# A chunked delta-rule attention with a top-1 expert layer behind it: the chunk loop as one written list, all triangular inverses in halves, routing for four chunks at a time

## The chip, the cores and the metric

One core of one Trainium2 chip. The metric is the time on the device in microseconds, from the first to the last instruction of one launch, as the median of several executions.

## What is computed

Inputs r, k, v, w, a, b have the shape 4 x 8 x 768 x 40 (batch, head, step, width). For each of the 32 (batch, head) pairs a 40 x 40 state runs over the 768 steps; the output of a step is read before its update:

```python
y[:, :, t] = np.einsum('bhd,bhde->bhe', rt, state)
Sa = np.einsum('bhde,bhe->bhd', state, at)
state = state * wt[:, :, None, :] - np.einsum('bhd,bhe->bhde', Sa, bt) + np.einsum('bhd,bhe->bhde', vt, kt)
```

The 3072 rows y (320 wide, all heads of a step side by side) go through a mixture of experts: `logits = x @ w_gate`, the largest of 8 logits picks one expert, and the output row is its softmax weight times `relu(x @ w1[e]) @ w2[e]`, with hidden width 1024.

## The kernel before

**Attention.** The 768 steps are cut into 24 chunks of 32. Two batches share the partitions (rows 0 to 39 and 64 to 103), and 16 pairs lie side by side in the free dimension. One chunk needs these stages; the letters are those of the orders in the code.

- Preparation `p` (`prep`): `scan` (L224, VectorE) makes running products of the decays, `inv` (L229, L230, ScalarE) their reciprocals by Ln and Exp, `gmul` (L241, L242, VectorE) refines these into G, `kbmul` (L235) scales k and b, and `qmul` (L246) makes Q from a and G; these last two run on GpSimd. It also issues the loads of the next chunk's W, k/b and a on SyncE's queue.
- Gram blocks `E` (`estage`, L255, TensorE): products of the scaled k, b with Q; ScalarE copies them out (`m2` L263, `m1` L275, L276), GpSimd masks half of them (L281).
- Inversion `tops`: for four chunks together, 32 x 32 unit triangular matrices, one for each pair and chunk, are inverted on VectorE. For the first four chunks only the two 16 x 16 diagonal halves are inverted so, in 14 steps of two operations (L309, L311), and TensorE joins them (`tbd`, L337, L347). For the other five groups all 32 rows are done in 30 steps of two operations (L301, L303). A copy puts each chunk's inverses into a block-diagonal tile TBD (L331, ScalarE).
- The recurrence, chunk after chunk: `R` (`rhs`, L375) multiplies the state with Q, ScalarE copies (L378), `U` (`ustage`, L385) applies the inverses, ScalarE copies (L390), `S` (`sstage`, L402) makes the next state, VectorE scales it out of PSUM into SVR (L408), and `R` of the next chunk reads that.
- Output: transposes `K` (L360), `T` (L415) and `u` (L425), products `A` (L441, masked by VectorE in L444) and `y` (L463, scaled into xT in L469).
- Routing, for two chunks at a time: `r` (`route_a`) makes the logits and the token rows, `b` (`route_b`) the ranks within each expert; two indirect DMAs on GpSimd (L538) scatter the rows, each behind the one before it, to a table Xs in DRAM that is laid out by expert.

Chunks 0 to 3 are issued by the list `START`, in which `wn` stands for n products on the constant `scn` whose result nobody reads. From chunk 4 on each chunk is issued by the one-line `ORDER`, with shares of the inversion steps between its stages; there the framework's scheduler may still move instructions within its own model of time. `YW` and `AW` put more products on `scn` before `y` and `A` (L448). All engines work off their queues in order.

**Experts.** For each of 8 experts, 448 rows are read from Xs and transposed, weights and rows are split into a high and a low part, and TensorE does the two layers (`l1` L877 to L882, `l2` L897 to L905). In `l1`, the last third of the contraction is 64 rows deep: L880 covers high weight times high and low row (stacked in x2), and L882 adds low weight times high row, two column blocks side by side on the upper and the lower 64 rows of the array. Results are scaled (L910, or L907 and L908 for the last 64 rows) and scattered to the output by an indirect DMA (L911). At the end a check of the decays and the expert counts decides whether a slow general path is needed, which is not the case here.

Of the kernel before, what the change touches and what calls it, by code (L numbers as in the profile page):

```python
# [42 lines left out]
START = ("W0 s0 l0 j0 W1 s1 a1 a0 w22 c0 k1 w12 l1 g0 Q0 g1 W2 s2 l2 q1 W3 s3 w9 c5 g2 a2 q2 l3 e0 w3 n0 e1 k2 w1 W4 "  # L43
# [9 lines left out]
ENGS = {mybir.EngineType.PE, mybir.EngineType.Activation, mybir.EngineType.DVE, mybir.EngineType.Pool,  # L53
        mybir.EngineType.SP}
INIT = {0: (0, 1), 1: (2, 3, 4), 2: (5, 6)}
AALT = 4
I0 = 4
# [4 lines left out]
NKB, NG = 9, 10  # L62


def prepare(inputs):
# [7 lines left out]
    W = np.zeros((NC, 80, 16, C + 1), f32)  # L73
    W[..., 1:] = em(w)
# [4 lines left out]
    VR[..., 0:40], VR[..., 64:104] = V[..., 0::2, :], V[..., 1::2, :]  # L79
# [36 lines left out]
    d["cq"] = np.broadcast_to((ii[None] == (jj % C)[:, None])[:, None, 0:16], (128, 8, 16)).astype(f32)  # L116
# [7 lines left out]
def attention(tc, nc, d, ctx, Xs, okt, sent):  # L124
# [325 lines left out]
    def ystage(c):  # L450
# [7 lines left out]
        for js in ((0, 1),) if c < NC - 1 else ((0,), (1,)):  # L458
# [6 lines left out]
            if js[0] == 0:  # L465
                yield
# [621 lines left out]
```

## Time and profile before

| what | value |
|---|---|
| median of 3 runs | 705.46 us (701.49 to 706.08) |
| profiled execution | 701.49 us, its span 701.5 us |
| busy share of the span | TensorE 86%, VectorE 76%, ScalarE 60%, GpSimd 33% |
| first product of stage U of chunk 0 / of chunk 23 | 65.1 us / 438.1 us |
| first product of the experts | 464.85 us |
| granted TensorE clock, mean | 0.879 |

The profile gives for each engine the busy time, and for groups of instructions the mean duration and what ended the idle time before them. Times in the views by stage are microseconds from the start of the span. TensorE's records are pipelined and overlap, so that its busy time is not the same as work at full rate.

### The profile page before, as it was taken

The numbers are of one execution on the slowest core, as the hardware profiler recorded it, in microseconds if no ns is written. First come the engines' busy times: TensorE is split into PE (matmuls) and PEld (weight loads), VectorE is DVE, ScalarE is ACT, GpSimd is POOL, SyncE is SP. The second block draws the span as 40 slices with busy tenths as digits, with TensorE's granted clock in tenths as the row PEclk, the third lists the DMA queues.
The fourth block names the chain that finished last, engine by engine and source line by source line (L and its number), as shares of the span: only waits on it lengthen the run. The fifth ranks groups of instructions, "written<-read, shape, count | busy, mean of one in ns | idle before, by whom it ended". The sixth has DMA issues, their size and how long they took to land. (4 is left out here: it accounts for less than half of the span.)

```text
span 701.5 us, 25718 instructions
## 1 busy us (share of the span) xinstructions
PE 601.3 (86%) x10942; PEld 510.3 (73%) x10942; DVE 535.8 (76%) x1074; ACT 422.9 (60%) x962; POOL 228.7 (33%) x239
## 2 busy tenths in 40 slices
PE   7477786877978877868889899889999999999994
PEld 3345565766867676757778788758898898988984
DVE  7999699998999999999789634558657576485531
ACT  2565755678759867978786887445535445355320
POOL 5860534546545544457312101200111101201101
PEclk9788767897877788888889989869999999999998
DMA  6484457253434343424224332886454464552100
GB/s 200 119 210 121 141 180 254 75 161 111 123 103 121 103 122 103 133 90 129 78 82 128 111 93 82 243 245 212 134 174 127 145 220 129 168 189 74 56 1 31
DMA packets 48207, 93.26 MB, mean 133 GB/s; under 512 B 11577, under 2 KB 28090, under 8 KB 48024
## 3 DMA queue, kind: packets, MB, share of 16 engines
q1 hardware_dynamic: 45528, 83.65, 39.9%
q0 software_dynamic: 2560, 7.92, 3.2%
q8 instruction: 88, 1.44, 0.9%
q14 instruction: 31, 0.25, 0.1%
HBM read 78.98 MB, written 13.21 MB: 131 GB/s over the span
## 5 line engine op out<-in xcount | busy, mean ns | idle before, releaser
L911 POOL DMA_INDIRECT out<-yo,tok x32 | 30.8, 964 | 207.6 <-DVE yo L910 149.8
L301 DVE TENSOR_TENSOR tmp<-Mt,Tt 128x30 f32<-128x30 f32 (+9 forms) x150 | 79.7, 532 | 2.8
L303 DVE TENSOR_TENSOR Tt<-Tt,tmp 128x30 f32<-128x30 f32 (+9 forms) x150 | 77.1, 514 | 3.2
L886 DVE SCALAR_TENSOR_TENSOR hx<-m_hp,hx 128x384 fp32r<-128x384 f32 (+1 forms) x128 | 41.0, 383 | 34.9 <-ACT hx L884 34.9
L246 POOL TENSOR_TENSOR Q<-AT,G 128x1024 f32<-128x1024 f32 x18 | 50.3, 2796 | 40.9 <-DVE G L242 14.0
L884 ACT ACTIVATE hx<-m_hp 128x448 fp32r<-128x448 f32 x64 | 31.4, 543 | 49.0 <-PE m_hp L882 44.8
L897 PE MATMUL m_yp<-w2h,hx 128*128 128x320 f32 x192 | 61.0, 317 | 0.0
L899 PE MATMUL m_yp<-w2h,hx 128*128 128x320 f32 x192 | 59.1, 308 | 0.0
L898 PE MATMUL m_yp<-w2l,hx 128*128 128x320 f32 x192 | 59.1, 308 | 0.0
L402 PE MATMUL ps_r<-SVS,KS 128*40 128x40 f32 x1472 | 49.8, 228 | 9.3 <-ACT SVS L390 6.2
L364 ACT COPY KS<-ps_g 64x416 f32<-64x416 f32 x96 | 48.1, 501 | 14.8 <-PE ps_g L360 10.0
L281 POOL TENSOR_SCALAR_AFFINE_SELECT Q<-Q 32x512 f32<-32x512 f32 x44 | 38.1, 865 | 57.4 <-ACT Q L275 50.1
L255 PE MATMUL ps_g<-Q,KB 128*64 128x64 f32 x768 | 38.4, 273 | 20.9 <-POOL Q L246 10.5
L463 PE MATMUL psY<-Y,KS 128*40 128x32 f32 x1504 | 50.4, 221 | 5.2 <-DVE Y L444 4.3
L402 PEld LDWEIGHTS ps_r<-SVS,KS 128*40 128x40 f32 x1472 | 44.1, 141 | 12.3 <-ACT SVS L390 8.6
L255 PEld LDWEIGHTS ps_g<-Q,KB 128*64 128x64 f32 x768 | 34.4, 183 | 25.5 <-POOL Q L246 11.9
L331 ACT COPY TBD<-Tc 32x256 f32<-32x256 f32 x80 | 50.8, 635 | 3.2 <-DVE Tc L314 1.3
L463 PEld LDWEIGHTS psY<-Y,KS 128*40 128x40 f32 x1504 | 44.9, 142 | 10.0 <-DVE Y L444 6.7
L408 DVE TENSOR_TENSOR SVR<-ps_r,F 40x320 f32<-40x320 f32 x92 | 44.9, 488 | 8.8 <-PE ps_r L402 6.2
L877 PE MATMUL m_hp<-x,w1h 128*128 128x448 f32 x128 | 50.1, 391 | 0.4 <-ACT x L860 0.4
L538 POOL DMA_INDIRECT Xs<-xr,si x24 | 27.9, 1164 | 61.5 <-ACT TBD L331 15.9
L878 PE MATMUL m_hp<-x,w1h 128*128 128x448 f32 x128 | 47.7, 373 | 0.0
(187 smaller groups left out, 1555.2 us busy)
## 6 DMA issues: line engine op xcount, KB each, us to landing
w2r<-in_w SPq DMA_DIRECT2D x8, 1280.0 KB
w1r<-in_w SPq DMA_DIRECT2D x8, 1024.0 KB
VU<-in_VT SPq DMA_DIRECT2D x48, 160.0 KB
SVR<-in_VR SPq DMA_DIRECT2D x48, 104.0 KB
SVS<-in_VS SPq DMA_DIRECT2D x24, 208.0 KB
KB<-in_KB SPq DMA_DIRECT2D x30, 160.0 KB
KB<-in_KBP SPq DMA_DIRECT2D x9, 512.0 KB
Xs<-xr SPq DMA_DIRECT2D x7, 648.0 KB
```

Of the source, the lines that this page charges most:

```text
L246: eng.tensor_tensor(at(Q, s), buf(s)[3], g, ALU.mult)
L255: TE.matmul(e[j][:, x], kb[:, p, :], q[:, :, p, :], start=True, stop=True, tile_position=(0, 64 * j))
L301: V.tensor_tensor(t, Mt[:, 0:j, j:j + 1].broadcast_to([128, j, n]), Tt[:, j:j + 1, j + 1:32].broadcast_to([128, j, n]), ALU.mult)
L303: V.tensor_tensor(Tt[:, 0:j, j + 1:32], Tt[:, 0:j, j + 1:32], t, ALU.subtract)
L331: A.copy(o[bb:bb + 32, :, bb:bb + 32], t[bb:bb + 32, :, n0:n0 + 8].rearrange("p i n->p n i"))
L364: A.copy(ks[0:64, u * 8 + z:u * 8 + 8:2], ts[u][64 * z:64 * z + 64])
L402: TE.matmul(s[TR[ty], x], ks[:, p, o:o + 40], sv[:, p, o:o + 40], start=True, stop=True, tile_position=(0, o))
L463: TE.matmul(py[TR[ty], p], ks[:, p, o:o + 40], y2[:, ty, p, :], start=True, stop=True, tile_position=(0, o))
L877: TE.matmul(hp, w1h[:, k, s], xh[:, k], start=k == 0, stop=False)
L897: TE.matmul(yp, hh[:, ft, qs], w2h[:, ft], start=ft == 0, stop=False)
L898: TE.matmul(yp, hh[:, ft, qs], w2l[:, ft], start=False, stop=False)
L899: TE.matmul(yp, hl[:, ft, qs], w2h[:, ft], start=False, stop=ft == 7)
```

## The change

**One list.** `START` becomes short (four preparations and the first inversion) and the new `ORDER` is one list of about 700 entries for all 24 chunks: `Xn` issues the next part of stage X of chunk n, `t` one inversion step. It is issued as written on all engines; the scheduler moves nothing. `TAIL` issues what is left of chunk 23. No products on `scn` stand in the list; 85 remain in `START` (140 before) and 5 in `YW` and `AW` (36 before).

**Preparation.** `inv` and `gmul` go. G comes from a reciprocal of the 16 full products and a second scan that runs backwards over W. `kbmul` and `qmul` of every chunk are on VectorE. G is a ring of 11 (10 before), and a chunk's `p` has two parts.

**Inversion.** Every group is inverted in halves, 14 steps of two operations; GpSimd clears the entries that must be zero (six memsets and a diagonal, per group). `B` (`merge`) joins the halves for every chunk: 32 products, four ScalarE copies, 16 products, one copy. TBD and its copies go; `U` reads the inverses where they lie.

**Two-head products.** `R` takes both batches of a pair at once: 16 products with 80 columns instead of 32 with 40. `S` writes a PSUM tile of its own, and VectorE empties it with two operations instead of four.

**Routing** runs once for four chunks (5 times for four, twice for two); the four scatters of a group wait for the group before, not for each other.

**Experts.** L882 becomes one product per column block over all 128 rows (`x2` holds high and low row, so low weight times low row is added as well); the copy into x3 goes. The last expert's row blocks run in the order 0, 1, 3, 2, the block that ends last leaves by one ScalarE operation, the output scatters do not wait for each other, and the check is made before the end.

```diff
-ORDER = ".05 R A T U b E .2 S .2 y C u K r .5 p 2 B"
+ORDER = ("y0 B0 B1 B0 M3 M2 j4 q4 i0 A0 B0 B0 p5 U0 p5 p6 E5 B1 U0 S0 E5 p6 K0 E5 B2 i1 S0 p7 E4 K0 B1 u0 p7 E4 B2 E4  "
...
-YW = tuple((c < 16) + (c == NC - 1) + 5 * (c in (5, 11, 17)) for c in range(NC))
+YW = tuple(int(c == NC - 1) for c in range(NC))
...
     def scan(s):
...
+        V.tensor_tensor_scan(f.rearrange("p a b->p (a b)"), w[:, 0:528], scn, 0.0, ALU.mult, ALU.max)
+        V.reciprocal(RC[:, 33:WN:33], f[:, :, 32])
+        V.tensor_tensor_scan(back(at(G, s)), back(w), back(RC), 0.0, ALU.mult, ALU.max)
...
-    def gmul(s):
-        _, f, nt, _ = buf(s)
-        g = at(G, s)
-        V.tensor_tensor(g, f[:, :, 1:], nt, ALU.mult)
-        V.scalar_tensor_tensor(g, g, 2.0, nt, ALU.subtract, ALU.mult, reverse0=True)
...
-        for j in range(14 if k < 1 else 30, 0, -1):
...
+        return [(2, first)] + [(2 * (0.12 + 2 * j * (15 - j) / 960), lambda j=j: step(j)) for j in range(14, 0, -1)] + [
+            (3.1, last)]
...
+    def merge(c):
+        t, m, n0 = at(Tc, c // 4), flat(at(ML, c // 4)), c % 4 * 8
         quads = [slice(bb, bb + 32) for bb in range(0, 128, 32)]
+        q = g4([128, 8, 32])
         for x in range(8):
+            h = n0 + x // 2 * 2
             for b in quads:
+                TE.matmul(q[b, x], m[b, (n0 + x) * 16:(n0 + x) * 16 + 32], Tc2[b, :, h:h + 2].rearrange("p a n->p n a"),
                           start=True, stop=True, tile_position=(b.start, b.start))
         yield
         for b in quads:
+            o = b.start % 64 + 16
+            A.copy(Q1[b, :, o:o + 16].rearrange("p (h l) a->p h l a", l=2), mine(q[b], 16))
+        yield
+        z = g4([128, 8, 64])
         for x in range(8):
+            h = n0 + x // 2 * 2
+            for b in (slice(0, 64), slice(64, 128)):
+                TE.matmul(z[b, x], Q1[b, x], t[b, h:h + 2].rearrange("p n a->p (n a)"), start=True, stop=True,
                           tile_position=(b.start, b.start))
         yield
+        A.copy(t[:, n0:n0 + 8, 0:16].rearrange("p (h l) a->p h l a", l=2), mine(z, 32))
...
         for h in range(8):
+            for j in range(2):
                 p = j * 8 + h
+                TE.matmul(psS[64 * j:64 * j + 64, h, 0:80], q[:, p].rearrange("e t i->e (t i)"),
+                          sr[:, :, h, j * 64:j * 64 + 40], start=True, stop=True, tile_position=(0, 64 * j))
...
+    def step_prep(s):
+        if s < NC:
+            scan(s)
+            if s + 1 < NC:
+                load_w(s + 1)
+            yield
+            kbmul(s, V)
+            qmul(s, V)
+            if s + 1 < NC:
+                load_a(s + 1)
...
+    for g in range(0, len(sent), 4):
+        for i in range(g, g + 4):
+            for j in range(g, i):
+                tc.declare_no_dep(sent[i].ins, sent[j].ins, reason="they write different rows")
...
-        for r, hp, s, x in zip((slice(0, 64), slice(64, 128)), hps, fs, (x2, x3)):
-            TE.matmul(hp, w1l[r, 2, s], x[r, 0], start=False, stop=True)
+            TE.matmul(hp, w1l[:, 2, s], x2[:, 0], start=False, stop=True)
```

VectorE in the middle of the loop, before: the inversion steps (tmp, Tt), the scaling of the state (SVR), the refinement of G and the scan.

```order
L303 TENSOR_TENSOR Tt<-Tt,tmp 128x25x6
L408 TENSOR_TENSOR SVR<-ps_r,F_112 40x4x2x40 x2
L242 SCALAR_TENSOR_TENSOR G_100<-G_100,nt 128x512
L224 SCALAR_TENSOR_TENSOR FF<-Wt,scn 128x528
L301 TENSOR_TENSOR tmp<-Mt,Tt 128x168
L303 TENSOR_TENSOR Tt<-Tt,tmp 128x24x7
L301 TENSOR_TENSOR tmp<-Mt,Tt 128x184
```

VectorE in the middle of the loop now: two scans with a reciprocal between them (L245 to L247), the shorter inversion steps (L311, L313), the state in one operation for each batch pair (L398).

```order
L245 SCALAR_TENSOR_TENSOR FF<-Wt,scn 128x528
L246 RECIPROCAL RC<-FF 128x16
L247 SCALAR_TENSOR_TENSOR G_92<-Wt,RC 128x528
L459 TENSOR_TENSOR xT<-psY,G_94 104x2x8x32
L311 TENSOR_TENSOR tmp<-Tt 128x100
L313 TENSOR_TENSOR Tt<-Tt,tmp 128x2x10x5
L398 TENSOR_TENSOR SVR<-psS,F_113 40x8x2x40 x2
```

The steps of up to 240 elements between the loop's other work have become steps of at most 112, and there are 28 of them for a group, not 60.

GpSimd in the middle of the loop, before: the products Q (L246) and KB (L235) stand between the masks (L281) and the scatters (L538).

```order
L538 DMA Xs<-xr,si 3584x324
L246 TENSOR_TENSOR Q_90<-AT,G_91 128x1024
L235 TENSOR_TENSOR KB_73<-KB_73,FF 128x1024
L236 COPY F_112<-FF 128x16
L281 AFFINE_SELECT Q_90<-Q_90 32x512 x2
```

GpSimd there now: scatters by four (L543), masks (L294), small copies and the memsets of the inversion (L301 to L304).

```order
L543 DMA Xs<-xr,si 3584x324 x4
L492 COPY xr<-cg 128x2
L493 MEMSET xr 128x2x2
L255 COPY F_113<-FF 128x16
L294 AFFINE_SELECT Q_88<-Q_88 32x16x32 x2
```

Both products have left GpSimd's queue; they are now in VectorE's, as the second part of each preparation.

TensorE around stage U of a chunk, before: A (L441), T (L415), U (L385), then y (L463) mixed with E (L255).

```order
L441 MATMUL ps_g<-RT,VU 64x2x32 x16
L415 MATMUL ps_g<-ident,SVR 104x40 x16
L385 MATMUL ps_r<-rs,TBD 32x40 x32
L463 MATMUL psY<-Y_104,KS_123 40x32 x6
L528 MATMUL ps_g<-gt,cg 128x16
L255 MATMUL ps_g<-Q_86,KB_85 64x64 x15
```

TensorE around a U now: R (L369), T (L405), the second product of a merge (L344), u (L415), U (L379), E (L268), A (L431), S (L393).

```order
L369 MATMUL psS<-SVR,Q_90 64x80 x16
L405 MATMUL ps_g<-ident,SVR 104x40 x16
L344 MATMUL ps_g<-Tc_116,NB 64x64 x16
L415 MATMUL ps_g<-ident,SVS 104x32 x16
L379 MATMUL psU<-RS,Tc_116 32x40 x32
L268 MATMUL ps_g<-Q_84,KB_83 64x64 x16
L431 MATMUL ps_g<-RT,VU 64x2x32 x16
L393 MATMUL psS<-SVS,KS_123 40x40 x32
```

Between R and U, where the copy of R's result is awaited, stand T, half a merge and u; between U and S stand E and A.

More of the change, by code (lines that the diff above doesn't have):

```diff
@@ L285, in first @@
         def first():
-            V.transpose(flat(Mt), M2c[0].rearrange("p n t->p t n"))
-            if k < 1:
-                A.copy(ML[:, 0:32], M2c[0][:, :, 0:16])
-        def second():
-            if k < 1:
-                d_ = lambda x: bass.AP(x.tensor, x.offset, [x.ap[0], [528, 2], [32, 16], [1, 16]])
-                V.tensor_tensor(d_(Tt), d_(Mt), d_(nm), ALU.mult)
-            else:
-                V.tensor_tensor(Tt, Mt, nm.rearrange("p (a b)->p a b", b=32), ALU.mult)
-            V.memset(flat(Tt)[:, 0:1024:33], -1.0)
@@ L315, in last @@
-            if k < 1:
-                V.transpose(flat(Tc2), Tt.rearrange("p a b->p b a")[:, 16:32])
-        o = [(1.2, first), (1.2, second)]
-        for j in range(14 if k < 1 else 30, 0, -1):
-            if k < 1:
-                o.append((2 * (0.075 + 2 * j * (15 - j) / 960), lambda j=j: step2(j)))
-            else:
-                o.append((2 * (0.075 + j * (31 - j) / 960), lambda j=j: step(j)))
-        o.append((1.2, last))
-        return o
-    def tbd(c):
-        t, n0, o = Tc[0], (c % 4) * 8, at(TBD, c)
-        if c >= 4:
-            for bb in range(0, 128, 32):
-                A.copy(o[bb:bb + 32, :, bb:bb + 32], t[bb:bb + 32, :, n0:n0 + 8].rearrange("p i n->p n i"))
-            return
+            V.transpose(flat(Tc2), Tt.rearrange("p a b->p b a")[:, 16:32])
@@ L348, in tbd @@
                           tile_position=(b.start, b.start))
         yield
-        for b in quads:
-            A.copy(o[b, :, b.start:b.start + 16], z[b])
+        A.copy(t[:, n0:n0 + 8, 0:16].rearrange("p (h l) a->p h l a", l=2), mine(z, 32))
     def kbt(c):
@@ L509, in route_a @@
         V.tensor_tensor(oh, oh, bc(km), ALU.is_equal)
-        if c < NC - 1:
+        if not last:
             G_.tensor_copy(a2[:, 0], acc)
-            G_.tensor_tensor(a2[:, 1], acc, oh[:, 0], ALU.add)
-            G_.tensor_tensor(acc, a2[:, 1], oh[:, 1], ALU.add)
-        G_.tensor_copy(xr[:, :, DM], cg[:, 296 + c - 1:298 + c - 1])
-        G_.memset(xr[:, :, DM + 2:XW], 0.0)
-        return xr, ex, oh, a2, se, sl
-    def route_b(st, last=False):
-        xr, ex, oh, a2, se, sl = st
-        rk = g4([128, 2, 8])
+            for i in range(n):
+                G_.tensor_tensor(acc if i == n - 1 else a2[:, i + 1], a2[:, i], oh[:, i], ALU.add)
+        ids()
+        yield
+        rk = g4([128, n, 8])
         if last:
@@ L581, in step_a @@
         if i < NC:
-            load_rt(i) if i == 0 else None
+            pass
         if 0 <= i - 1 < NC:
@@ L777, in attention @@
-    for _ in step_route_b(NC):
-        pass
-    for i in range(1, 4):
-        for j in range(i + 1, 5):
-            tc.declare_no_dep(sent[-i].ins, sent[-j].ins, reason="they write different rows")
-        tc.add_manual_dep(sent[-i].ins, sent[-5].ins.name, mybir.DependencyInfo(
-            mybir.DependencyClass.Sync, mybir.DependencyReason.DATA))
+                    for t in ML:
+                        G_.memset(flat(t)[:, 512:544], 0.0)
+                    DMA.dma_start(Q1, d["cq"])
+    once = {"j": lambda s: kbmul(s, V), "q": lambda s: qmul(s, V), "M": m1_mask}
@@ new lines, in attention @@
+    groups, to, gens = iter(range(1, NC // 4)), [], {}
+    for op in ORDER.split():
+        if op == "t":
+            if not to:
+                to = tops(next(groups))
+            to.pop(0)[1]()
+            continue
+        if op == "f":
+            hot = g4([128, 512])
+            for _ in range(2):
+                TE.matmul(hot, scn[:, 0:128], scn[:, 0:512], start=True, stop=True)
+            continue
+        if op[0] in once:
+            once[op[0]](int(op[1:]))
+            continue
+        if op not in gens:
+            gens[op] = steps[op[0]](int(op[1:]))
+        next(gens[op], None)
@@ new lines, in attention @@
+    gens = {}
+    manual.__exit__(None, None, None)
+    for i in (NC, NC + 1):
+        with tc.manual_schedule(engines={mybir.EngineType.PE}):
+            for step in TAIL.split():
+                if step == "b":
+                    for _ in gens.pop("r", ()):
+                        pass
+                elif step == "r" and i == NC:
+                    gens["r"] = step_route(i)
+                    for _ in range(3):
+                        next(gens["r"])
+                elif step != "r":
+                    for _ in steps[step](i):
+                        pass
@@ L945, in moe @@
                 load_w(e + 2)
-            for q in range(4):
+            for i, q in enumerate((0, 1, 2, 3) if e + 1 < E else (0, 1, 3, 2)):
                 if e + 1 < E:
                     list(xprep(e + 1, q))
+                elif i > 1:
+                    verdict(i == 3)
                 l2(e, q)
```

397 lines of the change are left out of this document (174 added, 223 removed), and 31 rows, old and new, of tables (ORDER, START).

## The prediction

> **What bounds the kernel now.** I read the busy time by stage first. Columns: length of the stretch, busy time of PE, weight loads, VectorE, ScalarE and GpSimd (with counts), granted clock, DMA share, GB/s. I cut the span where the first U of chunk 0 starts, where the inversions thin out, at the last U and at the experts.
>
> ```profile
> 0.00:65.10 65.10, 44.33 (x507) 24.23 (x507) 58.90 (x77) 31.21 (x71) 37.60 (x37) 0.84 0.63 167
> 65.10:340.80 275.70, 221.21 (x6041) 190.91 (x6040) 258.70 (x492) 203.39 (x478) 139.90 (x133) 0.81 0.43 128
> 340.80:438.10 97.30, 88.30 (x2786) 79.01 (x2784) 63.28 (x176) 78.30 (x177) 15.67 (x33) 0.89 0.33 98
> 438.10:464.80 26.70, 20.58 (x313) 15.96 (x311) 14.55 (x34) 11.96 (x27) 4.68 (x4) 0.79 0.76 221
> 464.80:691.60 226.80, 226.71 (x1300) 200.10 (x1300) 139.19 (x294) 97.51 (x213) 29.93 (x31) 0.99 0.44 139
> 691.60:701.50 9.90, 0.19 (x2) 0.11 (x2) 1.15 (x6) 0.52 (x1) 0.92 (x1) 0.72 0.07 22
> ```
>
> The products of U alone, 64 records a chunk, in the second and third of these stretches:
>
> ```profile
> 65.10:340.80 275.70, 15.65 (x960) 13.24 (x960) 0.81 0.43 128
> 340.80:438.10 97.30, 7.88 (x512) 6.79 (x512) 0.89 0.33 98
> ```
>
> So 15 chunks take 275.7 us (18.4 each), and 8 take 97.3 (12.2 each). In the first stretch VectorE is busy 94% and nothing else comes near; in the second TensorE is busy 91%, ScalarE 80%, VectorE 65%. The experts are TensorE from end to end. The groups of VectorE in the first stretch, and the two largest inversion groups in the second:
>
> ```profile
> L301 DVE TENSOR_TENSOR tmp<-Mt,Tt 128x30 f32<-128x30 f32 (+14 forms) x118 | 69.2, 586 | 2.1
> L303 DVE TENSOR_TENSOR Tt<-Tt,tmp 128x30 f32<-128x30 f32 (+14 forms) x118 | 66.9, 567 | 2.5
> L408 DVE TENSOR_TENSOR SVR<-ps_r,F 40x320 f32<-40x320 f32 x60 | 29.3, 488 | 2.8 <-PE ps_r L402 1.0
> L224 DVE TENSOR_TENSOR_SCAN FF<-Wt,scn 128x528 f32<-128x528 f32 x16 | 19.9, 1245 | 0.1
> L444 DVE TENSOR_TENSOR Y<-ps_g,mask 64x512 f32<-64x512 f32 x28 | 19.0, 680 | 1.5 <-PE ps_g L441 1.2
> L242 DVE SCALAR_TENSOR_TENSOR G<-G,nt 128x512 f32<-128x512 f32 x17 | 11.6, 684 | 0.2
> L469 DVE TENSOR_TENSOR xT<-psY,G 104x512 f32<-104x512 f32 x14 | 9.4, 675 | 0.8 <-PE psY L463 0.8
> L286 DVE STREAM_TRANSPOSE Mt<-M2c 128x1024 f32<-128x1024 f32 x4 | 7.9, 1976 | 3.6 <-ACT M2c L263 3.6
> ```
> ```profile
> L301 DVE TENSOR_TENSOR tmp<-Mt,Tt 128x58 f32<-128x58 f32 (+14 forms) x32 | 10.5, 330 | 0.7
> L303 DVE TENSOR_TENSOR Tt<-Tt,tmp 128x84 f32<-128x84 f32 (+14 forms) x33 | 10.5, 318 | 0.7
> ```
>
> The same steps take 586 and 567 ns on average early and 330 and 318 late. The order of time shows why: two steps that stand over 2 us, and what GpSimd does meanwhile.
>
> ```profile
> 257.44 2.53 DVE L303 TENSOR_TENSOR Tt<-Tt,tmp 128x228 f32<-128x228 f32 x1
> 260.00 2.25 DVE L301 TENSOR_TENSOR tmp<-Mt,Tt 128x220 f32<-128x220 f32 x1
> ```
> ```profile
> 257.32 2.39 POOL L246 TENSOR_TENSOR Q<-AT,G 128x1024 f32<-128x1024 f32 x1
> 259.68 2.33 POOL L235 TENSOR_TENSOR KB<-KB,FF 128x1024 f32<-128x1024 f32 x1
> ```
>
> Each step ends with the GpSimd product that began before it or beside it: some 2 us lost per product. The Trainium skill's SBUF — State Buffer (Who interferes with whom) says that a VectorE instruction with two SBUF inputs is fully blocked by a GpSimd instruction that reads SBUF; these rows agree.
>
> **VectorE's part of the change.** Prices from rows:
>
> ```profile
> L311 DVE TENSOR_TENSOR Tt<-Tt,tmp 128x108 f32<-128x108 f32 (+6 forms) x9 | 2.7, 302 | 0.3
> L309 DVE TENSOR_TENSOR tmp<-Mt,Tt 128x112 f32<-128x112 f32 (+6 forms) x8 | 1.9, 243 | 0.2
> L246 DVE TENSOR_TENSOR Q<-AT,G 128x1024 f32<-128x1024 f32 x2 | 2.4, 1202 | 0.0
> L316 DVE STREAM_TRANSPOSE Tc<-Tt 128x512 f32<-128x512 f32 x1 | 1.0, 1000 | 0.0
> ```
>
> The list holds five inversions. Each is 28 operations at 0.27 (mean of L309 and L311), 7.6 us, with transposes of 1.98, 1.0 and between 1.0 and 1.98: 12.2 each, 61 in all, where L301 and L303 alone take 157.1 today (69.2 + 66.9 + 10.5 + 10.5). A preparation is two scans at 1.245, a small reciprocal (0.2) and two products at 1.20: 5.1. The backward scan reads float32 twice and has no row of its own; from below it is a plain pass over 512 elements (0.68), from above twice the scan, and I take the scan, which has the same length and serial form. The 18 preparations behind the first U come to 92. The state leaves by 46 operations of 640 elements: 0.82 each by the slope between 320 (0.488) and 1024 elements (1.202), at most 0.98, so 38 to 45. L444 and L469 stay, 23 chunks x (2 x 0.68 + 0.68) = 47. The routing shrinks to about 11 (six sets of ten operations of some 0.18). The sum is 249 to 256 us for 23 chunks against 322.0 busy today: 11 a chunk. Masks and memsets on GpSimd still collide, which I put between 0 and 15 us; 11.3 a chunk.
>
> **ScalarE.** 281.7 us today over these 23 chunks:
>
> ```profile
> L331 ACT COPY TBD<-Tc 32x256 f32<-32x256 f32 x80 | 50.8, 635 | 3.2 <-DVE Tc L314 1.3 <-PE ps_r L385 0.2
> L229 ACT ACTIVATE nt<-FF 128x512 f32<-128x512 f32 x20 | 12.7, 633 | 14.2 <-DVE FF L224 14.0
> L351 ACT COPY TBD<-ps_g 32x128 f32<-32x128 f32 x16 | 4.1, 257 | 7.8 <-PE ps_g L347 7.6
> ```
>
> L331 goes (-50.8), so do L229 and its like-sized partner (about 18 x 1.27 = -23). Added for 23 merges are five copies of L351's size or its length (0.26): +30; the wider copy behind R costs up to +0.4 a chunk. That leaves 238 to 247, 10.5 a chunk.
>
> **TensorE** gains work. Runs of products at full clock:
>
> ```profile
> 380.85 0.80 PE L385 MATMUL ps_r<-rs,TBD 128*32 128x40 f32 x64
> 378.66 0.88 PE L375 MATMUL ps_r<-SVR,Q 128*32 128x40 f32 x58
> 390.00 1.15 PE L441 MATMUL ps_g<-RT,VU 128*64 128x64 f32 x32
> ```
>
> In the third stretch a chunk holds nearly all stages but E, and TensorE is busy 88.3 / 8 = 11.0. Now E is added in 20 of 23 chunks (1.15, as A, whose shape it has: +1.0), a merge in each (0.80, as U, and 0.80 to 1.15: +1.6 to +1.95), and R with 80 columns (between 0.88 and 1.15 x 80 / 64 = 1.44: +0 to +0.56). So 13.6 to 14.5 a chunk, of which part is waiting inside the runs of S and y. TensorE is now the fullest engine, not VectorE. The fillers that go are these, between the first and the last U:
>
> ```profile
> L448 PE MATMUL psY<-scn 128*128 128x512 bf16 x31 | 11.7, 457 | 0.0
> ```
>
> That is 0.5 us a chunk at most. I credit nothing: they stand where the products of y wait for the masking of L444 (0.68 us), so that wait hid them.
>
> **The period.** Before, one engine was 94% busy at 18.4 us, and 91% at 12.2. Now three engines at 11.3, 10.5 and about 14 stand side by side, all in order, with a chain R, copy, U, copies, S, scaling through all of them. 14.0 at 0.97 busy gives 14.5, and that is my value; 13.6 at full use less the waits inside gives 13.0 from below; from above 14.5 / 0.91 = 15.9. VectorE's cover is thin: where p5 to p8 follow each other, a scan waits for the load of W into the one buffer, behind 2.4 us of products. The first such load of the span:
>
> ```profile
> L193 SPq DMA_DIRECT2D Wt<-in_W x40: 281/319/1404, 1.5 to 304.4; - x40
> 4.26 1.26 DVE L224 TENSOR_TENSOR_SCAN FF<-Wt,scn 128x528 f32<-128x528 f32 x1 [0.48 <-DMA Wt<-in_W]
> 7.28 1.23 DVE L235 TENSOR_TENSOR KB<-KB,FF 128x1024 f32<-128x1024 f32 x1 [1.76 <-DMA KB<-in_KBP]
> ```
>
> It takes 4.26 - 1.5 = 2.8 us, so each of these pairs may lose 0.4 us, more when other loads stand ahead of it on SyncE's queue; masks, Gram products and merges of that chunk wait behind it. That lies inside the 15.9.
>
> **The start.** From 7.28 VectorE has the products of chunk 0 (2.4), three preparations (15.3), a memset and a fifth pair of scans (3.2), a transpose, four masks (3.7), the 28 steps and two transposes (10.2): 42.1. Behind that stand half a merge and U's wait, 1.5 to 2: 44 if every load is in time, 65.1 if the order gains nothing. I take 47, since the loads of this stretch already keep the DMA engines 63% busy.
>
> **The experts.** Around L882, one of 32 times:
>
> ```profile
> 677.49 0.37 PE L879 MATMUL m_hp<-x,w1l 128*128 128x448 f32 x1
> 677.70 0.37 PE L880 MATMUL m_hp<-x,w1h 128*128 128x448 f32 x1
> 678.00 0.47 PE L882 MATMUL m_hp<-x,w1l 64*128 64x448 f32 x2
> 678.40 0.42 PE L897 MATMUL m_yp<-w2h,hx 128*128 128x320 f32 x1
> ```
>
> From L880 to the next product behind L882 pass 0.70 us. L879 and L880, whole products, start 0.21 apart; three at about that spacing need 0.61, so 0.09 x 32 = 2.8 us go. The copy into x3 was hidden behind products: nothing. The end loses one operation, under 1 us: not counted. Between the last U and the experts (26.7) the chain of transposes, A, y, routing, scatter and reading back is the same; the scatters that no longer wait for each other lie before it.
>
> **The sum.** 47 + 23 x 14.5 (333.5) + 26.7 + 224.0 + 9.9 = 641.1 us against a span of 701.5. The profiled execution is the fastest of the three shown; their median is 705.46, 0.56% above, so 641.1 becomes **644 us**.
>
> **The rivals.**
> *Packed.* Fine interleaving lets TensorE run without waits, 12.5 a chunk: 47 + 287.5 + 260.6 = 595, as a median 598. For it: VectorE and ScalarE need only 11. Against it: with 91% busy TensorE needed 12.2 for less work.
> *The list stalls.* In-order engines of equal load wait for each other, PSUM buffers (four now for all transposes, merges, E and A) and loads, and the mean period stays at today's 373 / 23 = 16.2: 47 + 373 + 260.6 = 680.6, median 684. For it: three engines with so much work never ran side by side here.
> *Slower: the clock.* Without fillers TensorE may be granted less. The stretch with VectorE as bound had 0.81 with them, the TensorE-bound one 0.89. Equality is reached at (701.5 - 47 - 260.6) / 23 = 17.1 us a chunk, that is, if 13.0 us of work at full clock ran at 0.76 or less and TensorE set the pace; at 0.70 it is 18.6 a chunk, 47 + 427 + 260.6 = 735, median 739. Against it: TensorE will be fuller than in either stretch. The Trainium skill's TensorE: Matmul & The Clock Gate (Why this matters for your kernels) warns of halved clock after idle gaps of some 3 us, which speaks against dropping fillers; the two granted clocks agree that a fuller TensorE is throttled less.
>
> **Chances and range.** The forecast (13.4 to 15.8 a chunk, 619 to 675) gets 0.60, packed 0.16, stalls 0.17, the clock 0.04, and 0.03 is left for about no change. A measurement of this kernel tells 1% from none. Faster by over 1%: 0.93; within 1%: 0.03; slower: 0.04. The range reaches into both neighbours, 606 to 684.
>
> **What would show it.** First U at 44 to 50; steps of L311 and L313 near 0.27 us with none over 1 us; TensorE over 90% busy between the first and the last U, its granted clock 0.9 or more; 3 us less in the experts. Wrong if VectorE is again the fullest engine, if U to U exceeds 16 us, or if the clock lies under 0.8.

## The result, and the profile after

The changed kernel took **646.2 us** (median of 4, 643.35 to 648.42) against 703.8 for the kernel before: a ratio of 0.922 (95%: 0.916 to 0.928). The prediction said 644. Later, beside the experiments, the same file took 671.2 us on one chip and 671.6 on another, with the kernel before at 705.7 and 705.1 beside it: 0.952 (0.944 to 0.959) and 0.953 (0.947 to 0.959). That is inside the predicted range, 27 us from the predicted value. Both have to be explained; experiments 1 to 4 are compared with the 671.2, experiments 10 to 12 with the 671.6, and 6 to 8 with the kernel before. Two single runs, 685.1 us in the second experiment and 682.3 in the fourth, fell into a slower state that executions of a kernel sometimes show, and the medians below leave them out.

First the busy time by stage of the first measurement, cut as in the prediction, with the sixth chunk's U (145.5) as a further cut. Columns: length, busy time of TensorE, weight loads, VectorE, ScalarE, GpSimd (counts), granted clock, DMA share, GB/s.

```profile
0.00:46.90 46.90, 32.45 (x409) 18.29 (x413) 43.08 (x68) 15.76 (x41) 13.41 (x29) 0.96 0.77 193
46.90:391.60 344.70, 306.57 (x9822) 280.11 (x9824) 246.25 (x419) 244.37 (x656) 86.76 (x166) 0.93 0.46 136
46.90:145.50 98.60, 82.13 (x2580) 75.13 (x2580) 83.69 (x118) 70.36 (x190) 21.50 (x48) 0.90 0.63 189
391.60:416.30 24.70, 19.95 (x327) 15.79 (x327) 14.59 (x35) 12.68 (x30) 4.96 (x5) 0.86 0.68 201
416.30:635.50 219.20, 219.01 (x1301) 206.83 (x1302) 141.23 (x299) 91.08 (x181) 29.65 (x31) 1.00 0.47 148
```

Of the 57.4 us between the two spans, the start gave 18.2 (65.1 to 46.9), the 23 chunks 28.3 (373.0 to 344.7, 15.0 a chunk), the way to the experts 2.0 and the experts with the end the rest, about 9. TensorE is now the fullest engine of the loop (89%), VectorE and ScalarE are busy 71% each. VectorE's and ScalarE's groups in the loop:

```profile
L398 DVE TENSOR_TENSOR SVR<-psS,F 40x640 f32<-40x640 f32 x46 | 37.8, 822 | 31.5 <-PE psS L393 30.7
L247 DVE TENSOR_TENSOR_SCAN G<-Wt,RC 128x528 f32<-128x528 f32 x19 | 25.4, 1338 | 0.7
L254 DVE TENSOR_TENSOR KB<-KB,FF 128x1024 f32<-128x1024 f32 x19 | 24.3, 1278 | 0.1
L245 DVE TENSOR_TENSOR_SCAN FF<-Wt,scn 128x528 f32<-128x528 f32 x19 | 23.8, 1253 | 5.2 <-DMA Wt<-in_W 5.1
L259 DVE TENSOR_TENSOR Q<-AT,G 128x1024 f32<-128x1024 f32 x19 | 23.6, 1243 | 1.5 <-DMA AT<-in_A 1.5
L313 DVE TENSOR_TENSOR Tt<-Tt,tmp 128x28 f32<-128x28 f32 (+6 forms) x70 | 17.5, 250 | 2.8
L311 DVE TENSOR_TENSOR tmp<-Tt 128x28 f32<-128x28 f32 (+6 forms) x70 | 16.8, 240 | 1.8
L338 ACT COPY NB<-ps_g 32x128 f32<-32x128 f32 x92 | 23.6, 257 | 6.2 <-PE ps_g L333 4.4
```

These are the prices of the prediction: steps at 0.25 us (0.27), the state at 0.82 an operation (0.82), products at 1.24 to 1.28 (1.20), merge copies at 0.257 (0.26). Only the backward scan was unknown, and it costs 1.34, not twice the forward one. VectorE is waiting for TensorE now: 30.7 us before L398, the scaling of the state, where before the same operation (L408) waited 1.0 us in the 15 chunks of the long stretch.

The loop of the second measurement, and of the third, in the same columns:

```profile
47.50:408.90 361.40, 316.51 (x9819) 286.83 (x9820) 248.16 (x419) 244.00 (x656) 88.65 (x166) 0.91 0.43 130
```
```profile
46.30:416.20 369.90, 322.01 (x9818) 291.40 (x9818) 248.19 (x418) 243.89 (x656) 83.95 (x166) 0.89 0.43 127
```

The work of VectorE and ScalarE is the same to 1%. TensorE's busy time grows as its granted clock falls: busy time times clock is 285, 288 and 287 us, so 12.4 to 12.5 us a chunk at full clock in all three. Of the 16.7 us by which the second loop is longer, 9.9 are this busy time. The other 6.8 are time in which TensorE is not busy, mostly in front of products that come late though no wait is shown. In the second measurement, around one U (at full speed 64 products take 0.79 us):

```profile
334.32 0.78 PE L379 MATMUL psU<-RS,Tc 32*32 32x40 f32 x37
335.57 0.28 PE L379 MATMUL psU<-RS,Tc 32*32 32x40 f32 x4 [0.47 <-issue]
336.35 0.27 PE L379 MATMUL psU<-RS,Tc 32*32 32x40 f32 x4 [0.51 <-issue]
337.11 0.27 PE L379 MATMUL psU<-RS,Tc 32*32 32x40 f32 x4 [0.49 <-issue]
```

Four products come, then nothing for half a microsecond, with no releaser named ("issue"). In the waits of TensorE (us in total, times, longest), the line for such gaps of U, over the whole loop of the first measurement and behind the sixth chunk of the second and the third:

```profile
PE psU L379 <- issue: 0.7, 1, 0.7
```
```profile
PE psU L379 <- issue: 6.7, 13, 1.1
```
```profile
PE psU L379 <- issue: 7.2, 14, 1.2
```

The order of time shows that the gaps come first and the lower clock behind them. In the records of all these runs the granted clock is either full or half, and the means above are mixtures of the two: 2 x (1 - 0.93) x 344.7 = 48 us of the first loop ran at half clock, 65 of the second and 81 of the third. Around the U shown above, in the columns of the first table:

```profile
331.00:334.30 3.30, 3.23 (x72) 3.00 (x71) 0.94 (x6) 2.69 (x7) 0.06 (x1) 1.00 0.02 5
334.30:337.40 3.10, 1.61 (x53) 1.02 (x49) 2.75 (x8) 0.16 (x1) 2.49 (x3) 1.00 0.51 167
337.40:344.20 6.80, 4.81 (x59) 4.16 (x60) 1.87 (x7) 3.52 (x9) 1.80 (x5) 0.50 0.29 96
344.20:347.50 3.30, 3.30 (x143) 3.26 (x142) 0.69 (x1) 0.68 (x2) 0.00 (x0) 0.99 0.05 16
```

With the first gaps TensorE is busy 52% of the time at full clock; then comes half clock for 6.8 us. Such gaps stand at the same four places in the second and the third measurement, in S of chunks 6 and 10 and in U of chunks 18 and 22. Each time they begin at full clock, and half clock begins within 4 us. In the first measurement there is one gap of this kind in the four places together.

### The profile page after: what moved, and what is told of

Same layout as the page of the kernel before. It is cut to its first block, busy times and chain, and to the rows that moved or that the text cites. A ratio compares the mean times of both kernels' runs of the same rounds, so it can differ in the third digit from the quotient of the medians.

```text
span 644.1 us, 27239 instructions
## 1 busy us (share of the span) xinstructions
PE 578.3 (90%) x11855; PEld 521.1 (81%) x11860; DVE 445.2 (69%) x818; ACT 364.4 (57%) x907; POOL 135.8 (21%) x232
## 4 chain that ended last, share of the span: by engine, by line
PE 63%; DVE 12%; issue 8%; ACT 8%; DMA 7%; POOL 1%; SPq 0%; POOLq 0%; DVEq 0%; ACTq 0%
PE m_yp L882 4%; PE m_yp L880 4%; PE m_yp L881 4%; PE psS L393 4%; PE m_hp L862 4%; PE m_hp L861 4%; PE m_hp L863 4%; PE psY L448 3%; PE psS L369 3%; PE ps_g L344 3%; PE ps_g L431 3%; PE ps_g L333 3%; PE ps_g L415 2%; PE ps_g L356 2%; DMA w2r<-in_w 2%
## 5 line engine op out<-in xcount | busy, mean ns | idle before, releaser
L294 POOL TENSOR_SCALAR_AFFINE_SELECT Q<-Q 32x512 f32<-32x512 f32 x46 | 46.6, 1014 | 69.9 <-ACT Q L289 65.4
L880 PE MATMUL m_yp<-w2h,hx 128*128 128x320 f32 x192 | 61.0, 317 | 0.0
L398 DVE TENSOR_TENSOR SVR<-psS,F 40x640 f32<-40x640 f32 x46 | 37.8, 822 | 31.5 <-PE psS L393 30.7
L882 PE MATMUL m_yp<-w2h,hx 128*128 128x320 f32 x192 | 59.3, 309 | 0.1
L434 DVE TENSOR_TENSOR Y<-ps_g,mask 64x512 f32<-64x512 f32 x48 | 32.9, 684 | 34.1 <-PE ps_g L431 33.6
L276 ACT COPY M2c<-ps_g 32x256 f32<-32x256 f32 x96 | 35.0, 364 | 26.1 <-PE ps_g L268 24.9
L861 PE MATMUL m_hp<-x,w1h 128*128 128x448 f32 x128 | 46.9, 367 | 0.4 <-ACT x L845 0.4
L863 PE MATMUL m_hp<-x,w1l 128*128 128x448 f32 x128 | 46.7, 365 | 0.0
L393 PE MATMUL psS<-SVS,KS 128*40 128x40 f32 x1472 | 39.7, 216 | 7.7 <-issue 6.4
L384 ACT COPY SVS<-psU 32x320 f32<-32x320 f32 x96 | 40.1, 418 | 7.7 <-PE psU L379 5.7
L393 PEld LDWEIGHTS psS<-SVS,KS 128*40 128x40 f32 x1472 | 35.2, 130 | 11.1 <-issue 7.7
L360 ACT COPY KS<-ps_g 64x320 f32<-64x320 f32 x96 | 40.4, 421 | 6.3 <-PE ps_g L356 3.8
L409 ACT COPY KS<-ps_g 40x320 f32<-40x320 f32 x92 | 38.6, 419 | 5.8 <-PE ps_g L405 4.0
L268 PE MATMUL ps_g<-Q,KB 128*64 128x64 f32 x768 | 31.6, 243 | 10.9 <-DVE Q L259 6.5
L369 PE MATMUL psS<-SVR,Q 128*64 128x80 f32 x768 | 35.6, 249 | 4.9 <-DVE SVR L398 3.6
L268 PEld LDWEIGHTS ps_g<-Q,KB 128*64 128x64 f32 x768 | 28.4, 155 | 14.1 <-DVE Q L259 7.9
L448 PE MATMUL psY<-Y,KS 128*40 128x32 f32 x1504 | 35.8, 206 | 2.7 <-issue 2.5
```

Source lines behind the costliest of these rows:

```text
L268: TE.matmul(e[j][:, x], kb[:, p, :], q[:, p], start=True, stop=True, tile_position=(0, 64 * j))
L294: G_.affine_select(q[o:o + 32, :, ty], q[o:o + 32, :, ty], pattern=[[0, 16], [-1, 32]], base=0, channel_multiplier=1, compare_op=ALU.is_gt ...
L369: TE.matmul(psS[64 * j:64 * j + 64, h, 0:80], q[:, p].rearrange("e t i->e (t i)"), sr[:, :, h, j * 64:j * 64 + 40], start=True, stop=True, ...
L393: TE.matmul(psS[TR[ty], h, j * 40:j * 40 + 40], ks[:, p, o:o + 40], sv[:, p, o:o + 40], start=True, stop=True, tile_position=(0, o))
L448: TE.matmul(py[TR[ty], p], ks[:, p, o:o + 40], y2[:, ty, p, :], start=True, stop=True, tile_position=(0, o))
L861: TE.matmul(hp, w1h[:, k, s], xh[:, k], start=k == 0, stop=False)
```

## The experiments

**1 to 4: one load added or one part undone.** In the first, the preparations of the list go back to GpSimd:

```diff
-            kbmul(s, V)
-            qmul(s, V)
+            kbmul(s, G_)
+            qmul(s, G_)
```

> The changed kernel, but the two products that scale k/b and Q of the 19 chunks prepared inside the list are on GpSimd again, as most were before. Theory (the products had to leave GpSimd because they hold up VectorE's operations with two inputs): VectorE is rid of 19 x 2 x 1.25 = 48 us, yet each of the 38 products of some 2.4 us costs neighbouring VectorE operations up to 2 us; the first six chunks, where nine preparations stand and VectorE is 85% busy, get 5 to 15 us longer, the whole 8 to 30 us slower than the changed kernel (654 to 676), and the mean of the inversion steps rises from 0.25 us to over 0.4 near the products. Rival (the written order alone brings the gain): VectorE loses 48 us of work, time 636 to 648.

Measured: 678.2 us, 0.958 of before (0.953 to 0.964), 7 us over the 671 of the changed kernel; the intervals of the ratios overlap, so that the difference is not told from none. VectorE's groups in its loop:

```profile
L247 DVE TENSOR_TENSOR_SCAN G<-Wt,RC 128x528 f32<-128x528 f32 x19 | 40.5, 2132 | 0.7
L245 DVE TENSOR_TENSOR_SCAN FF<-Wt,scn 128x528 f32<-128x528 f32 x19 | 29.8, 1568 | 13.3 <-DMA Wt<-in_W 11.9 <-POOL F L255 1.4
L313 DVE TENSOR_TENSOR Tt<-Tt,tmp 128x28 f32<-128x28 f32 (+6 forms) x70 | 24.7, 352 | 2.8
L311 DVE TENSOR_TENSOR tmp<-Tt 128x28 f32<-128x28 f32 (+6 forms) x70 | 22.1, 316 | 1.9
```

The holds are there: the backward scan rises from 1.34 to 2.13 us, the steps from 0.25 to 0.33. But these four groups gain 34 us (117 against 83.5) while 48 leave, and the first six chunks took 17.0 each, as in the second and third measurements (16.7, 17.1). It lies between the theory (8 to 30 slower) and the rival (at most 2 slower): if the move is worth anything, it is a few us.

The second adds products on TensorE ahead of every y:

```diff
-        busy(YW[c])
+        busy(5 + YW[c])
```

> The changed kernel with five products on the constant (128 x 512) ahead of the output products of every chunk, 23 x 5 more; 12 such products took 5.0 us and 31 took 8.93 us elsewhere in it, so 0.29 each where the clock is high, 1.4 us a chunk, 33 us in all. Theory (from the sixth chunk on TensorE sets the pace, 91% busy at 14.5 a chunk): 15 to 26 us slower (661 to 672), nearly all behind 145 us. Rival 1 (the chain through three engines sets the pace and TensorE waits in between): under 8 us slower. Rival 2 (idle TensorE is throttled, fillers raise the clock): granted clock between the first and the last U above 0.96 against 0.93 now, time 640 to 650.

Measured: 677.2 us, 0.959 (0.952 to 0.966): 6 us slower for some 33 us of added products, with intervals that overlap again. The theory (15 to 26) is out; the time is as rival 1 had it (under 8). About four fifths of the added work cost nothing, so it must have stood mostly in time in which TensorE waited. Rival 2 (640 to 650) is wrong in its time. Whether the added products raise the clock is not shown: over the span it was 0.940 to 0.947, against 0.913 to 0.929 in the unchanged kernel, but the fourth experiment, whose loop is the unchanged one, had up to 0.946.

The third repeats Q's product on VectorE (the same values again):

```diff
             qmul(s, V)
+            qmul(s, V)
```

> The changed kernel with the product that makes Q done twice on VectorE for the 19 chunks prepared in the list (the same values written again): 19 x 1.24 = 23.6 us more on VectorE. Theory (VectorE, with nine preparations in six chunks, sets the pace up to 145 us and TensorE behind it): 6 to 14 us slower, of which at least 5 in the first six chunks, and under 3 in the other seventeen. Rival 1 (TensorE everywhere): under 4 us slower in all. Rival 2 (the first six chunks wait for loads, which stand in SyncE's queue behind the filling of the table): under 4 in the first six chunks too.

Measured: 675.9 us, 0.955 (0.950 to 0.961): 4.7 us slower for 23.6 us of added work, between rival 1 (under 4) and the theory (6 to 14), and with intervals that overlap. By place, its first six chunks and the rest:

```profile
48.30:153.90 105.60, 87.03 (x2584) 78.99 (x2584) 95.93 (x126) 70.38 (x190) 23.79 (x48) 0.85 0.56 173
153.90:421.10 267.20, 239.73 (x7242) 217.47 (x7241) 177.44 (x311) 174.20 (x467) 65.65 (x118) 0.89 0.36 106
```

The first six chunks took 105.6 us, against 100.2 and 102.9 in the second and third measurements, with VectorE at 91%; the other seventeen 267.2, against 261.2 and 267.0. The two unchanged runs differ by more in the rest (5.8) than this run does from either in the first six chunks (5.4 and 2.7). So VectorE has little room in the first stretch, but what the added work cost there is not told from the spread.

The fourth restores the old third of the experts' first layer:

```diff
-            TE.matmul(hp, w1l[:, 2, s], x2[:, 0], start=False, stop=True)
+        for r, hp, s, x in zip((slice(0, 64), slice(64, 128)), hps, fs, (x2, x3)):
+            TE.matmul(hp, w1l[r, 2, s], x[r, 0], start=False, stop=True)
```

> The changed kernel with the old last third of the experts' first layer: low weight times high row as pairs of 64-row products on the upper and lower rows, and the copy into x3. As predicted the pairs cost 0.09 us each, 2.8 us in all (649). From the profile after, an expert takes 27.4 us instead of 28.2, which is twice that: 0.2 us a pair, 6 us in all (652). If the expert's period changed for another reason (the copy, the loads), it stays at 27.4 and the time at 646.

Measured: 671.5 us, 0.954 (0.946 to 0.962), the time of the changed kernel within the spread of the loop. The experts, which do not depend on the loop, say it exactly: from the first product of one expert to that of the next pass 28.17 us, against 27.45 in every run of the changed kernel. That is 0.72 x 8 = 5.8 us, near the 6 that the profile after had led to, and twice the prediction's 2.8.

Its loop, which the edit does not touch, also tells clock and gaps apart:

```profile
47.60:410.70 363.10, 313.26 (x9822) 282.87 (x9825) 248.13 (x418) 243.93 (x656) 86.49 (x166) 0.93 0.44 129
```

The clock is the 0.93 of the first measurement, and the loop is still 18 us longer. The gaps of the second and the third measurement are there, at the same four places and in U of chunk 15 (18 gaps before products of U, 8.9 us in all).

**5: the same kernel again.**

> The changed kernel itself once more, on the chip of the first four experiments. Those four took 674 to 680 us, also the one whose attention loop is untouched (363 us from the first to the last U where the first measurement had 345). If the loop's time depends on the edit, this run gives 643 to 650 as at first; if on the chip or the moment, 665 to 675, and the four have to be read against that.

671.2 us. The longer loop of the first four runs is not due to their edits; what the first measurement had and this one has not is told above.

**6 to 8: parts of the change in the kernel before.** Its order from chunk 4 on is left to the framework's scheduler, as it was. Sixth, the products of the loop on VectorE; seventh, all groups in halves (with the old join, 64 products a chunk); eighth, both.

```diff
-        kbmul(s, G_)
+        kbmul(s, V)
         gmul(s)
-        qmul(s, G_)
+        qmul(s, V)
```
```diff
-        for j in range(14 if k < 1 else 30, 0, -1):
+        for j in range(14, 0, -1):
...
-        if c >= 4:
+        if c >= NC:
```

> The kernel before with only one part of the change: in the preparations of the loop the two scaling products run on VectorE instead of GpSimd. Theory (GpSimd products hold up VectorE's two-input operations): 11 preparations add 2 x 1.2 = 26 us to VectorE and take away 22 holds of some 2 us = 44; VectorE sets the pace there, so 8 to 20 us faster than before (686 to 698), and the inversion steps fall from 0.58 to below 0.45 us on average. Rival (the holds cost nothing that counts): VectorE only gets fuller, 5 to 26 us slower (711 to 732).

> The kernel before with only another part: all groups inverted in halves, 28 operations a group instead of 60, and the halves joined by the old code of the first group (32 products, a ScalarE copy, four VectorE copies, 32 products, four ScalarE copies a chunk). Theory (VectorE at 94% sets the pace of chunks 0 to 14): the steps shrink from 157 us to some 45 (28 x 5 at 0.32), the joins add 20 x 1.2 = 24, so VectorE loses 88 of 322 us; the period of 18.4 falls to what TensorE and ScalarE allow, 14 to 15, some 11 chunks long: 35 to 50 us faster (655 to 670). Rival (without a new order the freed time is lost to waits): under 15 us faster (690 or more).

> The kernel before with both parts, halves for all groups and the two products on VectorE. Theory (both are VectorE's load): between 0 and 15 us faster than the halves alone, 645 to 665, so that list, two-head products and routing bring under 20 more. Rival (the order is the larger part): 675 or more.

Measured: 727.3 us (1.030, 1.022 to 1.037), 757.2 (1.075, 1.064 to 1.085) and 765.8 (1.085, 1.078 to 1.092). All three are slower, by 22, 52 and 60 us, where the theories had 8 to 60 faster; the time of the sixth is its rival's (5 to 26 slower), and those of the seventh and eighth lie on their rivals' side. And yet VectorE was relieved, as the steps of the sixth show; over the same loop of the kernel before they took (69.2 + 10.5) / 150 = 0.53 us and (66.9 + 10.5) / 151 = 0.51:

```profile
L303 DVE TENSOR_TENSOR Tt<-Tt,tmp 128x30 f32<-128x30 f32 (+9 forms) x150 | 61.1, 408 | 3.4
L301 DVE TENSOR_TENSOR tmp<-Mt,Tt 128x30 f32<-128x30 f32 (+9 forms) x150 | 56.5, 377 | 3.3
```

The first 15 chunks of the sixth, which took 275.7 us in the kernel before:

```profile
65.10:357.40 292.30, 219.78 (x6028) 191.50 (x6045) 249.10 (x524) 205.81 (x482) 99.68 (x114) 0.80 0.40 120
```

VectorE is busy 85% there, no longer 94%, so the rival's reason (VectorE only gets fuller) does not hold. TensorE has the same busy time as before (219.8 and 221.2) and is idle 18 us more. The whole loop of the seventh:

```profile
65.80:493.60 427.80, 356.61 (x11304) 315.08 (x11324) 268.39 (x616) 259.05 (x673) 145.99 (x166) 0.77 0.34 105
```

VectorE needs 268 us there instead of 322. TensorE got more to do: the old join adds some 2500 products, its busy time rises by 47 us (309.5 to 356.6) and its idle time by 8, at a clock of 0.77. So the seventh and the eighth move load as well as remove it. Nor is the order of the kernel before kept: the scheduler sorts the loop anew for each of the three, and in the sixth about 160 of VectorE's 1075 instructions stand in another order than before. What the three show is that less work on VectorE does not by itself make this loop faster when the scheduler orders it; relief in the old order, held fixed, was not tried.

**9 to 12: the order.** The ninth is the measure for the other three.

> The changed kernel a third time, as the measure for the three that run beside it. It took 646 us at first and 671 in the second session, with the kernel before at 704 and 706; between the two only the loop differs (345 and 361 us), by a lower granted clock (0.94 and 0.91 behind the sixth chunk) and by products of U that come late without any wait. 640 to 680; whichever of the two it is, the clock should go with it: 0.94 to 0.96 over the span at 646, 0.92 to 0.93 at 671.

671.6 us, clock 0.913 to 0.926. The tenth sorts the list's entries from chunk 5 on so that every stage stands in one piece:

```diff
-... R5 T5 R5 y4 p13 T5 U5 r4 A5 B6 p13 A5 U5 B6 r4 t S5 u5 y5 u5 S5 r4 B7 B7 R6 t y5 ...
+... R5 R5 p14 p14 t A5 A5 T5 T5 t U5 U5 B6 B6 E13 t E13 E13 u5 u5 S5 t S5 y5 y5 K5 t K5 R6 R6 ...
```

> The changed kernel with the entries of its list from chunk 5 on sorted into one plain order for every chunk, each stage in one piece (R, p, A, T, U, B, E, u, S, y, K, r, and the inversion steps spread evenly): the same instructions, not finely mixed. Theory, as it now stands (the mixing of stages keeps TensorE supplied, and parts of the change alone made the old order slower by 21 to 60 us): TensorE waits for each copy between R, U and S and for the two copies of each merge, 1 to 2.5 us more a chunk over 18 chunks, 20 to 45 us slower than the changed kernel beside it. Rival (the lighter VectorE and ScalarE alone make room, the order hardly matters once they have it): under 10 us slower.

In this order the load of k and b for nine chunks later comes before stage K has read that buffer, so K transposes other numbers; kinds and counts of instructions are the same, and TensorE waits for no such load before K. Measured: 749.9 us, 1.065 (1.056 to 1.073), 78 slower than the changed kernel beside it, well over the 20 to 45 expected. The second product of the merge now stands right behind its first:

```profile
L346 PE MATMUL ps_g<-Tc,NB 64*64 64x64 f32 x736 | 44.0, 281 | 34.3 <-ACT NB L340 23.1 <-DVE Y L436 10.0 <-ACT Q L291 0.3
```

The same line in the list of the first measurement:

```profile
L344 PE MATMUL ps_g<-Tc,NB 64*64 64x64 f32 x736 | 30.3, 235 | 2.3 <-issue 1.6 <-ACT NB L338 0.6
```

That is 32 us of new waiting in front of one line; for the rest of the 78 no single place is shown. The eleventh hands the list to the scheduler instead of issuing it as written:

```diff
+    manual.__exit__(None, None, None)
     once = {"j": lambda s: kbmul(s, V), "q": lambda s: qmul(s, V), "M": m1_mask}
...
     gens = {}
-    manual.__exit__(None, None, None)
```

> The changed kernel whose list is only the order in which instructions are handed to the framework's scheduler, which may move them by its own model of time, as it did before from chunk 4 on. TensorE's order differs in some 150 rows. Theory (an order fitted to this chip's waits): 5 to 25 us slower than the changed kernel beside it, with S's products split by products of the next merge. Rival (moves of a few products do nothing): within 5 us.

Measured: 767.1 us, 1.088 (1.078 to 1.097): **95 us slower**, with the same instructions, where 5 to 25 was expected. TensorE's own order is nearly the written one; about 160 of VectorE's 819 instructions and 100 of SyncE's 452 transfers stand elsewhere. On SyncE's queue the scheduler puts all seven fills of the table ahead of the first state, and loads of W and of k and b where its model needs them. Waits in the loop that grew or are new:

```profile
DVE KB L254 <- DMA KB<-in_KB: 30.3, 8, 5.2
DVE FF L245 <- DMA Wt<-in_W: 24.4, 8, 12.7
```
```profile
PE psS L369 <- DVE SVR L398: 19.2, 5, 7.6
PE ps_g L268 <- DVE Y L434: 13.7, 1, 13.7
```

(In us: total, times, longest.) Behind late loads VectorE prepares late, scales the state late, and R waits for it. The first U comes at 63.1 us, where it was before the change (65.1), not at 46.3 as in the ninth. The loops of the tenth and the eleventh:

```profile
47.30:486.00 438.70, 352.42 (x9838) 323.60 (x9838) 245.42 (x422) 246.50 (x659) 77.62 (x169) 0.79 0.35 106
```
```profile
63.10:511.70 448.60, 354.93 (x9792) 323.26 (x9790) 244.24 (x415) 244.86 (x653) 76.67 (x163) 0.79 0.30 90
```

Again 278 and 280 us of TensorE at full clock, but busy only 80% of the time and at 0.79. With 12.2 us of work a chunk, 12.2 / (0.79 x 0.79) = 19.5, which is the eleventh's period. At the clock of the first measurement its waits alone would give 12.2 / (0.79 x 0.93) = 16.6, an estimate from these rows. Where half clock follows stretches in which TensorE waits, as around the U above, waiting is paid twice, once as waiting and once as clock.

The twelfth moves the fills of the table to GpSimd's queue:

```diff
-        DMA.dma_start(Xs[i * n:(i + 1) * n].rearrange("(q p) x->p q x", p=128),
+        G_.dma_start(Xs[i * n:(i + 1) * n].rearrange("(q p) x->p q x", p=128),
```

> The changed kernel with the seven transfers that fill the table Xs (648 KB each) on GpSimd's queue instead of SyncE's, so that loads of W, a and v no longer stand behind them. Theory (the first six chunks take 16.4 us each, 2 more than the others, because VectorE waits 5.1 us for W at 57 us and 1.5 for a, and TensorE for what follows): 3 to 9 us faster than the changed kernel beside it, all before 150 us. Rival 1 (VectorE's nine preparations in six chunks set that stretch): within 3 us. Rival 2 (the transfers then collide with all loads at once): 2 to 8 us slower.

Measured: 673.6 us, 0.953 (0.946 to 0.961), as the ninth (671.6). VectorE's wait for W in the first stretch stays:

```profile
DVE FF L245 <- DMA Wt<-in_W: 5.3, 1, 5.3
```

The first six chunks take 103.5 us (102.9 in the ninth), as rival 1 had it. So the fills in SyncE's queue are not what makes these chunks longer. Rival 1's reason, VectorE's nine preparations, is not shown either: in the first experiment VectorE is busy only 75.8 of the 101.9 us there, and the stretch is no shorter.

## Why the prediction was right, and where it was not

**The start** (47, measured 46.9) held, and its reason too, with an addition: it needs SyncE's loads where the list writes them. In the eleventh, where the scheduler moved them, it is 63.1.

**The loads of the engines** held: VectorE 11.3 a chunk forecast, 246.25 / 23 = 10.7 measured (with 19 preparations behind the first U, not the 18 counted); ScalarE 10.5 and 10.6; TensorE 13.6 to 14.5 and 306.57 / 23 = 13.3, of it 12.4 at full clock. TensorE became the fullest engine, and its clock rose from 0.83 (0.81 and 0.89, weighted) to 0.93 with almost no fillers, as said against the clock rival. The Trainium skill's warning of a halved clock after idle gaps of some 3 us (TensorE: Matmul & The Clock Gate, Why this matters for your kernels) agrees with the halving, but the measurement goes further: of the nine stretches at half clock in the loop of the second measurement, two stand behind gaps over 3 us (4.4 and 3.8), and near the other seven no gap is over 2 us. The fillers were miscounted: the row shown (L448, 0.5 us a chunk) leaves out 26 more products on `scn` behind the first U, of `START` (L719, 9.5 us), which makes 0.9. The sum put both at nothing, and no run here tries the old fillers in the new loop.

**The period** was 14.5, measured 15.0, of which 14.5 behind the sixth chunk ((391.6 - 145.5) / 17) and 16.4 before it. In the later measurements it was 15.7 and 16.1, nearly the rival of the stalled list, and the last is past the 16 us that the prediction named as a sign of being wrong. The step that failed is "14.0 at 0.97 busy": it treated TensorE as the engine that sets the pace, so that work and time go one to one. TensorE is busy 89%, under the 90% that was to show it. 33 us more work on it cost about 6, and 23.6 more on VectorE 4.7. So neither engine sets the pace of the whole loop. The period is work at full clock (12.4) over the busy share (0.89) and the clock (0.93). That the value came out near is partly luck: the busy time was put too high (14.0, measured 13.3) and the busy share as well (0.97, measured 0.89), and the two errors largely cancel. Busy share and clock are what changed between the measurements.

**What brings the gain** was put in the wrong place. The sum was built from VectorE's relief (products off GpSimd, half the inversion steps); the order appeared only as a danger, the list that stalls at 16.2. The runs put the order first: the same instructions in two other orders lose 78 and 95 us, and are then 45 and 62 slower than the kernel before. Parts of the relief, in orders that the scheduler made for them, lose 22 to 60. The holds by GpSimd were read rightly from two pairs of rows and are real (1.34 to 2.13 us), but undoing the move costs about 7 us of 671, which is not told from none. The Trainium skill's rule in SBUF — State Buffer (Who interferes with whom) agrees with the held operations; neither it nor two neighbouring rows say what a hold is worth when the held engine has time to spare. So the order is needed for the gain; how much of it the order would bring alone stays open. Whether the new order alone, with the old 30-step inversions, would do was not tried: the list is written for the new parts.

**The experts** were mis-sized: 2.8 us forecast, 0.72 x 8 = 5.8 measured. The interval from L880 to the next product was counted, 0.09 too long. The product behind the pair is late as well; around the pair of another group of the kernel before:

```profile
561.58 0.37 PE L880 MATMUL m_hp<-x,w1h 128*128 128x448 f32 x1
561.88 0.47 PE L882 MATMUL m_hp<-x,w1l 64*128 64x448 f32 x2
562.28 0.47 PE L877 MATMUL m_hp<-x,w1h 128*128 128x448 f32 x1
562.59 0.36 PE L878 MATMUL m_hp<-x,w1h 128*128 128x448 f32 x1
562.79 0.36 PE L879 MATMUL m_hp<-x,w1l 128*128 128x448 f32 x1
```

From L877 to L878 pass 0.31 instead of 0.20. A change in the shape of products costs on the way in and on the way out: 0.09 + 0.10 = 0.19, times 32 is 6.1, near the 5.8. This error (3.0), the shorter way to the experts (24.7, not 26.7), a first expert of 28.4 instead of 30.8 us, 1.8 beyond its share of the pairs (27.8 to 30.1 in the later runs of the new experts, so not a gain to count on), and an end of 8.6 instead of 9.9 happened to pay for most of the longer period: 11.2 us over in the loop, 8.1 under behind it.

**Left open:** why the same file takes 646 in one session and 671 in another. Shown is where: TensorE's clock in the loop (0.93, then 0.91 and 0.89) and products that come late without a wait. At the four places that differ, the late products come before the half clock, and the fourth experiment has them at a clock of 0.93, so a lower clock is not what brings them. What starts them no run here tells. Two chips gave 671; on which chip the 646 was measured is not known, so a difference between chips is not ruled out. The kernel before stays at 704 to 706 throughout; that VectorE's pace in 15 of its 23 chunks hides the difference is an argument, not shown.

## What to carry to other kernels

Here, with three engines 70 to 90% full, their loads no longer gave the time; the order decided between 671 and 767 us. In such a case an experiment that only reorders the same instructions should come first, and the unchanged new kernel should be measured again beside every group of experiments. Sum the work of the fullest engine at full clock, and ask separately what busy share and what granted clock the order will reach. And count what a differently shaped product costs until the spacing is regular again, not to the next start.

## What the runs showed of the hardware that was not expected

TensorE's granted clock in the loop goes with how fully the order keeps it supplied, though loosely: 0.93 at 89% busy, 0.89 at 87%, but 0.93 at 86% in the fourth experiment; 0.77 at 83%, 0.79 at 80% and at 79%. The mean is a mixture of full and half clock. In the loop of the second measurement each of the nine stretches at half clock begins behind 3.4 us in which TensorE was busy 25 to 59%, mostly without a long gap. Extra products that nobody reads (33 us) cost about 6 us and did not show a clearly higher clock. Two measurements of one kernel, 25 us apart in two sessions, differed in TensorE's clock and in gaps of about 0.5 us after every four products of some U and S, at the same places of the program, which no wait explains, while VectorE and ScalarE did the same work in the same time.
